# A small 32-bit matmul ahead of the third plain unit, and a new order of work, in an attention and two-layer kernel

## The chip, the cores and the metric

The kernel runs on one core of a Trainium2 chip. A core has engines that run side by side, each with its own queue of instructions: TensorE (PE in the profile; PEld is its loading of weights), VectorE (DVE), ScalarE (ACT), GpSimd (POOL) and SyncE (SP), which here only issues transfers. Sixteen DMA engines move data between the memory (HBM) and the core. Engines wait for each other by semaphores; within one engine the instructions are done in the order of its queue. The metric is the time of one execution on the device, in microseconds.

## The reference

Causal attention over 24 heads of 448 positions with 64 columns each, then two layers on the 896 x 768 result: a gated one and one with hardswish.

```python
scores = scale * np.matmul(q, k.transpose(0, 1, 3, 2))
scores = np.where(mask, -1000000000.0, scores)
attn = np.exp(scores - max); attn = attn / (sum + 1e-09)
x = (attn @ v) as (896, 768)
gate = 1.0 / (1.0 + np.exp(-(x @ w_gate)))      # 768 x 1536
x = (gate * (x @ w_val)) @ w_out                # 1536 x 768
h = x @ w_in                                    # 768 x 2048
out = (h * np.clip(h + 3.0, 0.0, 6.0) / 6.0) @ w_out2   # 2048 x 768
```

The weights come as 64-bit floats.

## The kernel before

**Numbers.** A 64-bit weight is loaded as two 32-bit words and turned into a 32-bit float by one ScalarE and four VectorE operations (`dec_scale`, `dec_shift`, `dec_clamp`, `dec_join`, `dec_sign`; tiles `raw` and `b`). Each operand of a product is split into a high part `hi` and a rest `lo`, both in the type that the profile calls fp32r; a product takes three matmuls (hi·hi, hi·lo, lo·hi). A split is done by ScalarE and VectorE (`split`), or by two ScalarE operations and a transfer that adds, issued by GpSimd (`dma_split`).

**Stages.** Attention comes first. Then the gated layer: four "plain units" (a unit is 128 columns of `w_gate` or `w_val`; 36 matmuls of 448 columns into accumulator `m`, line 994 and before), after that ten pairs of units by a scheme with seven products instead of eight (`Pairs`), which needs sums of the operand: T1 to T4, made in `tsum` tiles r11, r12, r21, r22 by eight sums `t_op(0)` to `t_op(7)` on VectorE and split into tiles `T`. The first pair multiplies the operand `x` by weights `g` (18 matmuls), then T2 by a weight sum `S` split into `hi` and `lo`, and so on, into accumulators `w`. Then `w_out` (accumulator `m`, tiles `y`), sixteen units of `w2_in` as eight pairs, and `w2_out` in two halves of 384 output columns, c = 0 and c = 1. Each half has seven tiles of 128 rows (`po[t]`), finished in the order 0, 2, 4, 6, 1, 3, 5, copied to `osb` and stored: half 0 by one transfer of all seven, half 1 by one transfer for each tile.

Two places already have a matmul of 64 x 64 in 32 bits on an accumulator that the next product overwrites: before the first product of `w_out`, and before the T2 product of the first pair of `w2_in`.

**Order.** Attention is issued by due times written in the kernel. After it every call is only noted (`Later`) and issued at the end by two tables. The steps of the four engines other than TensorE are numbered, ScalarE's first, then VectorE's, GpSimd's and SyncE's (966 to 1032). `ORDER` lists these numbers; `AHEAD` says how many of TensorE's steps, which keep the order of the program, come before each. Each engine's queue follows the table. Of SyncE's numbers 1023 is the store of half 0, and 1026 to 1032 are the stores of half 1's tiles t = 0, 2, 4, 6, 1, 3, 5.

Of the kernel before, what the change touches and what calls it, by code (L numbers as in the profile page):

```python
# [70 lines left out]
def kernel(  # L71
# [12 lines left out]
    nc = tc.nc  # L84
    B, H, S, D = q.shape
# [175 lines left out]
    with tc.manual_schedule():  # L261
        kept = ctx.enter_context(tc.tile_pool(name="kept", bufs=1))
        tsum = [kept.tile([P, 2, HK, S], F32, tag=f"q{2 + i}", name="tsum") for i in range(2)]
        r11, r12 = (tsum[0][:, i] for i in range(2))
# [377 lines left out]
        nc = Later(nc)  # L642
# [347 lines left out]
        def plain_unit(j):  # L990
            f, v = divmod(j, 2)
            if j < 2:
                ps = first_acc[j]
                halves(ps, at1[f, v], x_of, 0, True, True, (1,))
            else:
                ps = acc()
                halves(ps, at1[f, v], x_of, 0, True, True)
            plain[v] = ps
# [87 lines left out]
        for o in range(KD):  # L1086
            py = acc()
            if o == 0:
                t = g1[0][0].bitcast(F32)[:, :D]
# [144 lines left out]
        for c in range(2):  # L1234
# [105 lines left out]
        )  # L1340
        AHEAD = (
# [71 lines left out]
```

## Time and profile before

| | |
|---|---|
| median of three runs | 574.07 us (573.53 to 575.9) |
| the profiled execution, its own time | 573.63 us |
| its span, first to last instruction | 571.9 us |
| PE / PEld busy | 565.2 us (99%) / 500.2 us (87%) |
| DVE / ACT / POOL busy | 462.9 us (81%) / 344.5 us (60%) / 92.5 us (16%) |
| granted clock of TensorE | 1.00 of full speed (2.4 GHz) |
| moved by DMA | 84.57 MB |

A busy share is an average over stages with different limits. Which stage is bound by what is read from the chain of waits, which is followed back from the last instruction, and from the timeline of one engine. Matmuls overlap, so the duration of one is longer than the distance from its start to that of the next; the distance is what counts in a stream of them, and it is got from the start times of groups. Records of matmuls and of weight loads stand apart, and the load for a matmul runs beside the matmul before it.

### The profile page before, as it was taken

Reading aid. Unit: us, or ns where it says so; the run is one execution under the profiler, and the core shown is the slowest. Engines: PE = TensorE matmul, PEld = TensorE weight load, DVE = VectorE, ACT = ScalarE, POOL = GpSimd, SP = SyncE. Lnnn points to the kernel's source line nnn. Section 1 sums busy time; section 2 is a strip of 40 time slices with the busy share of each in tenths; the row PEclk is TensorE's granted clock in tenths of the full one; section 3 lists DMA queues with packets and bytes.
Section 4 is the critical chain, followed back from the end, with each engine's and each line's share of the span. In section 5 each row is a group of like instructions: output and inputs, shape, how many; then the busy total and the mean of one; then the engine's idle time right before and its main releaser. Section 6 shows DMA issues by size and latency. Waiting matters only on the chain.

```text
span 571.9 us, 8667 instructions
## 1 busy us (share of the span) xinstructions
PE 565.2 (99%) x3220; PEld 500.2 (87%) x3221; DVE 462.9 (81%) x706; ACT 344.5 (60%) x648; POOL 92.5 (16%) x152
## 2 busy tenths in 40 slices
PE   9999999999999999999999999999999999999997
PEld 5666656899999999999999999999999999999997
DVE  4789998897988998899878779899989999858201
ACT  4888888296667566686334439868768764333100
POOL 2545646021111110100000002212111000000000
PEclk9999999999999999999999999999999999999999
DMA  7756650389767686752644456898988153336002
GB/s 157 164 141 146 149 144 18 108 184 229 204 154 168 160 245 166 180 153 41 198 157 147 150 140 111 195 219 209 231 202 197 45 166 111 118 104 207 0 14 84
DMA packets 87785, 84.57 MB, mean 148 GB/s; under 512 B 35776, under 2 KB 77504, under 8 KB 87744
## 3 DMA queue, kind: packets, MB, share of 16 engines
q1 hardware_dynamic: 79904, 64.27, 37.9%
q0 software_dynamic: 6912, 19.53, 19.2%
q8 instruction: 25, 0.41, 0.3%
q10 hardware_dynamic: 928, 0.23, 0.2%
q14 instruction: 16, 0.13, 0.1%
HBM read 61.73 MB, written 2.75 MB: 113 GB/s over the span
## 4 chain that ended last, share of the span: by engine, by line
PE 90%; DVE 6%; ACT 2%; issue 1%; POOL 0%; DVEq 0%
PE w L46 40%; PE m L46 40%; PE pav L441 2%; PE pt L421 2%; PE s L367 2%; ACT pr L391 1%; DVE nm L379 1%; PE tr L334 1%; PE pt L533 1%; PE m L240 1%; DVE tsum L280 1%; DVE b L175 1%; DVE pth L431 1%; DVE raw L167 1%; DVE b L181 1%
## 5 line engine op out<-in xcount | busy, mean ns | idle before, releaser
L46 PE MATMUL m<-hi,g 128*128 128x384 f32 x448 | 113.9, 334 | 0.0
L46 PE MATMUL w<-T,hi 128*128 128x448 f32 x324 | 92.1, 366 | 0.0
L46 PEld LDWEIGHTS m<-hi,g 128*128 128x128 f32 x448 | 81.0, 188 | 0.0
L46 ACT ACTIVATE b<-raw 128x768 f32<-128x768 f32 x62 | 56.3, 914 | 37.9 <-DVE lo L46 18.2
L46 PE MATMUL m<-lo,g 128*128 128x384 f32 x224 | 74.8, 334 | 0.0
L46 PE MATMUL m<-g,hi 128*128 128x448 f32 x288 | 70.2, 366 | 0.0
L46 PEld LDWEIGHTS w<-T,hi 128*128 128x128 f32 x324 | 60.8, 188 | 4.9
L46 DVE SCALAR_TENSOR_TENSOR b<-raw,b 128x768 int32<-128x768 int32 x62 | 58.9, 954 | 1.0
L46 DVE SCALAR_TENSOR_TENSOR b<-b,raw 128x768 int32<-128x768 int32 x62 | 58.8, 954 | 0.9
L46 PE MATMUL w<-T,lo 128*128 128x448 f32 x162 | 59.2, 365 | 0.0
L46 PEld LDWEIGHTS m<-g,hi 128*128 128x128 f32 x288 | 54.0, 188 | 4.3
L411 POOL TENSOR_SCALAR pr<-pr,rc 128x192 f32<-128x192 f32 (+3 forms) x96 | 48.7, 525 | 49.2 <-DVE rc L403 40.4
L46 POOL DMA_DIRECT2D lo<-S x34 | 30.4, 898 | 152.9 <-ACT lo L46 98.2
L391 ACT ACTIVATE pr<-s,nm 128x192 f32<-128x192 f32 (+3 forms) x96 | 44.7, 479 | 4.7 <-DVE rc L403 2.5
L46 ACT CAST hi<-b 128x768 fp32r<-128x768 f32 x28 | 23.5, 838 | 38.4 <-DVE b L46 27.2
L46 DVE TENSOR_SCALAR b<-b 128x768 f32<-128x768 f32 x62 | 34.2, 555 | 12.9 <-ACT b L46 12.6
L46 PEld LDWEIGHTS m<-lo,g 128*128 128x128 f32 x224 | 42.0, 188 | 0.0
L46 PE MATMUL m<-g,lo 128*128 128x448 f32 x144 | 40.9, 365 | 0.0
L46 DVE TENSOR_TENSOR lo<-b,hi 128x768 fp32r<-128x768 f32 x28 | 26.6, 954 | 16.5 <-ACT hi L46 16.2
L46 DVE TENSOR_SCALAR raw<-raw 128x768 int32<-128x768 int32 x62 | 34.5, 560 | 4.6 <-DMA raw<-in_moe_w_in_dram 2.1
L46 PE MATMUL w<-x,g 128*128 128x448 f32 x180 | 38.2, 365 | 0.0
L46 ACT CAST g<-b 128x384 fp32r<-128x384 f32 (+1 forms) x36 | 23.9, 675 | 20.8 <-PE w L46 11.2
(124 smaller groups left out, 1086.4 us busy)
## 6 DMA issues: line engine op xcount, KB each, us to landing
raw<-in_moe_w_out_dram SPq DMA_DIRECT2D x28, 768.0 KB, 4.6
lo<-S POOLq DMA_DIRECT2D x34, 384.0 KB, 4.3
raw<-in_moe_w_in_dram SPq DMA_DIRECT2D x16, 768.0 KB, 5.7
raw<-in_moe_w_gate_dram SPq DMA_DIRECT2D x12, 768.0 KB, 5.3
raw<-in_moe_w_val_dram SPq DMA_DIRECT2D x12, 768.0 KB, 4.9
g<-b POOLq DMA_DIRECT2D x9, 384.0 KB, 6.3
q<-in_q_dram SPq DMA_DIRECT2D x24, 112.0 KB, 3.6
k<-in_k_dram SPq DMA_DIRECT2D x22, 112.0 KB, 3.7
```

The source lines that it names most:

```text
L46: steps.append((name, lambda: fn(*args, **kw)))
L167: nc.vector.tensor_scalar(lower, lower, 29, None, op0=ALU.logical_shift_right)
L175: nc.vector.scalar_tensor_tensor(bi, bi, 3, words(u)[1], op0=ALU.logical_shift_left, op1=ALU.bitwise_or)
L181: nc.vector.scalar_tensor_tensor(bi, words(u)[0], -(2 ** 31), bi, op0=ALU.bitwise_and, op1=ALU.bitwise_or)
L240: nc.tensor.matmul(ps[:, b, :S], lhsT=w[a][:, i * P : (i + 1) * P], rhs=x(c, k0 + i, b), start=(first and i == 0 and n == 0), stop=(last a ...
L280: op(r, a.bitcast(F32), b.bitcast(F32))
L334: nc.tensor.transpose(ps[:, c * CP : (c + 1) * CP], t[:, c].rearrange("p j d -> p (j d)"), identf[:CP, :CP],)
L367: nc.tensor.matmul(live["s", p, t][:, j], lhsT=live["qt", p][r, Q0[t] : Q0[t] + P], rhs=live["kt", p][r, : Q1[t]], start=False, stop=True, ...
L391: nc.scalar.activation(to if j else to[:, ::-1], ps[:, j].rearrange("p (c d) -> p c d", d=D), AF.Exp, bias=nm[:, j : j + 1], accum_out=sm[ ...
L411: nc.gpsimd.tensor_scalar(pr[:, j], pr[:, j], rc[:, j : j + 1], 1.0, op0=ALU.mult, op1=ALU.mult)
L421: nc.tensor.transpose(ps[:, o : o + P], live["pr", p, t].rearrange("p j n -> p (j n)")[:, c : c + P], identf,)
L441: nc.tensor.matmul(pav[r, Q0[i] :] if i else pav, lhsT=x[:, j] if i else x.rearrange("p j d -> p (j d)"), rhs=pt[g][:, off : off + w], sta ...
```

## The change

Before the product of the third plain unit (j == 2) a small matmul is put on the same accumulator. It reads 64 columns of r11, a 32-bit tile, as both operands, and the product overwrites what it writes. The two tables are new as a whole; their last rows are shown.

```diff
             else:
                 ps = acc()
+                if j == 2:
+                    t = r11[:, 0, :D]
+                    nc.tensor.matmul(ps[:D, 0, :D], lhsT=t, rhs=t, start=True, stop=True)
                 halves(ps, at1[f, v], x_of, 0, True, True)
             plain[v] = ps
...
-            909, 914, 368, 369, 371, 370, 1026, 915, 1029, 916, 1030, 1027, 1031, 1028, 917,
-            1032,
+            370, 1027, 1028, 1026, 915, 916, 371, 1030, 917, 1031, 1032, 1029, 1023,
```

TensorE's queue differs by the one matmul, between the second and the third plain unit (`x_73` is the last quarter of the attention's result, `x_70` the first, `m` the accumulator):

```order
 L46 MATMUL m<-x_73,hi 128x448 x2
 L46 MATMUL m<-x_73,lo 128x448
+L46 MATMUL m<-tsum 64x64
 L46 MATMUL m<-x_70,hi 128x448
 L46 MATMUL m<-x_71,hi 128x448
```

Nothing else in that queue moves.

VectorE's queue at the same time, before the change (`tsum_79` holds r11 and r12, `tsum_80` r21 and r22; the four rows that write `tsum` from `tsum` are t_op(4) to t_op(7)):

```order
L46 TENSOR_TENSOR tsum_80<-x11_73 128x1344
L46 TENSOR_TENSOR tsum_80<-tsum_80,tsum_79 128x1344
L46 TENSOR_TENSOR S_1747<-b_82 128x384
L46 TENSOR_SCALAR raw_1718<-raw_1718 128x768
L46 TENSOR_TENSOR S_1748<-b_81,b_82 128x384
L46 TENSOR_TENSOR S_1747<-S_1747,b_81 128x384
L46 TENSOR_SCALAR b_1754<-b_1754 128x768
L46 TENSOR_TENSOR tsum_79<-tsum_79 128x1344
L46 TENSOR_SCALAR b_1782<-b_1782 128x768
L46 TENSOR_TENSOR tsum_79<-tsum_80,tsum_79 128x1344
L46 TENSOR_SCALAR raw_1720<-raw_1720 128x768
L46 TENSOR_TENSOR tsum_80<-tsum_80,tsum_79 128x1344
```

and with it (`raw1_0_1741<-m_1685` is the gate product of the first two plain units):

```order
L46 TENSOR_TENSOR tsum_80<-x11_73 128x1344
L46 TENSOR_TENSOR tsum_80<-tsum_80,tsum_79 128x1344
L46 TENSOR_TENSOR tsum_79<-tsum_79 128x1344
L46 TENSOR_TENSOR tsum_79<-tsum_80,tsum_79 128x1344
L46 TENSOR_SCALAR raw_1718<-raw_1718 128x768
L46 TENSOR_TENSOR S_1747<-b_82 128x384
L46 TENSOR_SCALAR b_1754<-b_1754 128x768
L46 SCALAR_TENSOR_TENSOR b_1754<-b_1754,raw_1718 128x768
L46 SCALAR_TENSOR_TENSOR b_1754<-raw_1718,b_1754 128x768
L46 TENSOR_TENSOR tsum_80<-tsum_80,tsum_79 128x1344
L46 TENSOR_TENSOR raw1_0_1741<-m_1685,raw1_0_1741 128x896
L46 TENSOR_SCALAR raw_1720<-raw_1720 128x768
```

t_op(5) and t_op(6), which writes r11 last, have moved ahead of the weight work and the weight sums `S`; the gate product has moved ahead of the rest of the sums.

ScalarE's queue around the end of the first pair's first product, before the change (`raw1_0_1741<-w_1777` is the copy of that product out of its accumulator, `lo_1787` and `lo_1791` are splits for the second pair):

```order
L46 ACTIVATE raw1_0_1741<-m_1749 128x896
L46 ACTIVATE lo_1787<-raw1_3_1760 128x768
L46 CAST g_1784<-b_1782 128x384
L46 ACTIVATE lo_1791<-raw1_3_1760 128x768
L46 COPY raw1_0_1741<-w_1777 128x448
```

and with it:

```order
L46 ACTIVATE raw1_0_1741<-m_1749 128x896
L46 CAST g_1784<-b_1782 128x384
L46 COPY raw1_0_1741<-w_1777 128x448
L46 CAST hi_1761<-S_1748 128x768
L46 ACTIVATE lo_1787<-raw1_3_1760 128x768
```

The copy now stands ahead of both splits.

The end of SyncE's queue (`128x7x384` is the store of half 0, `128x384` that of a tile of half 1, `raw<-...` loads of weights):

```order
 L46 DMA raw<-in_moe_w_in_dram 128x6x128 x14
-L46 DMA raw<-in_moe_w_out_dram 128x2x384 x15
+L46 DMA raw<-in_moe_w_out_dram 128x2x384 x16
+L46 DMA out_dram<-osb 128x384 x7
 L46 DMA out_dram<-osb 128x7x384
-L46 DMA raw<-in_moe_w_out_dram 128x2x384
-L46 DMA out_dram<-osb 128x384 x7
```

The store of half 0 has moved from before the last load to behind all seven stores of half 1.

## Rows read from the trace of the kernel before

**Rows 1.** Chain of waits, from attention's end: start us, us, what
```profile
105.19 5.77 PE m L240 x27
110.96 22.32 PE m L46 x108
133.28 127.75 PE w L46 x630
261.02 88.01 PE m L46 x434
349.03 102.60 PE w L46 x506
451.63 116.52 PE m L46 x672
...
568.25 0.56 DVE osb L46
```

**Rows 2.** Timeline of TensorE's matmuls: start us, us, engine, line, operation, out<-in, tile, count
```profile
118.24 0.99 PE L46 MATMUL m<-x,hi 128*128 128x448 f32 x4
...
119.48 0.99 PE L46 MATMUL m<-x,hi 128*128 128x448 f32 x4
...
133.12 3.88 PE L46 MATMUL w<-x,g 128*128 128x448 f32 x18
136.83 0.56 PE L46 MATMUL w<-T,hi 128*128 128x448 f32 x2
...
206.14 3.81 PE L46 MATMUL w<-x,g 128*128 128x448 f32 x18
209.79 1.99 PE L46 MATMUL w<-T,g 128*128 128x448 f32 x9
```

**Rows 3.** The same view around the two small matmuls of before
```profile
259.04 1.98 PE L46 MATMUL w<-T,g 128*128 128x448 f32 x9
260.95 0.33 PE L46 MATMUL m<-g 128*64 128x64 f32 x2
...
262.53 0.97 PE L46 MATMUL m<-g,hi 128*128 128x448 f32 x4
...
352.61 0.33 PE L46 MATMUL w<-hi 128*64 128x64 f32 x2
```

**Rows 4.** Timelines of ScalarE and of weight loads at the first T2 product
```profile
135.35 0.84 ACT L46 ACTIVATE lo<-raw 128x768 fp32r<-128x768 f32 x1
136.09 0.52 ACT L46 COPY raw<-w 128x448 f32<-128x448 f32 x1
...
136.66 0.36 PEld L46 LDWEIGHTS w<-T,hi 128*128 128x128 f32 x2
```

**Rows 5.** Timeline of VectorE: t_op(4) and t_op(6)
```profile
111.97 1.56 DVE L46 TENSOR_TENSOR tsum<-tsum 128x1344 f32<-128x1344 f32 x1
...
117.72 1.55 DVE L46 TENSOR_TENSOR tsum<-tsum 128x1344 f32<-128x1344 f32 x1
```

**Rows 6.** Timelines of GpSimd and VectorE; in brackets idle time before, and its releaser
```profile
128.18 0.83 POOL L46 DMA_DIRECT2D lo<-S x1 [0.77 <-ACT lo L46]
...
137.63 0.56 DVE L46 TENSOR_TENSOR g<-b,g 128x384 fp32r<-128x384 f32 x1 [2.29 <-DMA lo<-S]
```

**Rows 7.** Stores: issue times (ns min/median/max, first and last start); KB and us to landing
```profile
L46 SPq DMA_DIRECT2D out_dram<-osb x8: 332/362/464, 516.5 to 568.8; - x8
...
out_dram<-osb SPq DMA_DIRECT2D x1, 1344.0 KB, 8.3
out_dram<-osb SPq DMA_DIRECT2D x7, 192.0 KB, 1.9
```

**Rows 8.** GB/s from 567 to 572 us in 40 slices; windows, GB/s last
```profile
GB/s 0 0 0 0 86 356 381 344 393 357 356 369 369 136 0 0 0 0 0 0 0 209 356 393 381 222 12 0 0 0 0 0 0 0 0 0 0 0 0 0
...
522.00:523.00 1.00, 1.00 (x8) 1.00 (x7) 0.85 (x1) 0.12 (x1) 0.00 (x0) 1.00 1.06 401
523.00:524.00 1.00, 1.00 (x8) 1.00 (x7) 0.19 (x1) 0.78 (x1) 0.00 (x0) 1.00 1.06 399
```

196 rows, old and new, of tables (AHEAD, ORDER) are left out of this document.

## The prediction

> **What bounds the kernel now.** I read the chain of waits first, because it says which engine the end hangs on at each time. The reader is to see in [rows 1] that up to 105 us it hops between engines (attention; its pieces are left out there), and that from 105.19 us to 568.15 us it is TensorE alone, without one piece of another engine or of waiting between. Then come only the last copy of a result tile on VectorE (0.56 us) and the stores. So 463 of 571.9 us are matmuls back to back. A change in the order on VectorE and ScalarE can gain nothing there; it can only lose, if an operand comes late. What can still change are three things: the number of matmuls, the distance from one matmul to the next, and what follows the last one.
>
> Second the timeline of TensorE, for that distance. It has two levels for 448 columns. In the four plain units it is 1.24 us for six, 206.7 ns (118.24 to 119.48) [rows 2]; later it is 3.65 us for 18, 202.8 ns (206.14 to 209.79) [rows 2]. The chain says the same over long pieces: 22.32 us for 108 is 206.7 ns, 127.75 for 630, 88.01 for 434 and 102.60 for 506 are each 202.8 ns [rows 1]. The granted clock is 1.00 (2.4 GHz) throughout, so this is not the clock. The step from one level to the other lies at 136.8 us, at the first matmul of the product with T2. That product accumulates into a bank which ScalarE must first copy out: the copy runs from 136.09 to 136.61 us, behind a 0.84 us operation that is not urgent, and the weight load starts at 136.66 us [rows 4], 0.03 us after its turn: a load starts with the matmul before its own, here the last of 18, at 133.12 + 17 x 0.2067 = 136.63 us. I take it that this little hold-up of the load put the stream of loads and matmuls into the closer spacing. That is argued, not shown.
>
> Third the stores: which transfer is issued last, how long it takes to land, and what rate stores reach [rows 7, 8].
>
> **The change part by part.** The sums are made against the profiled execution: span 571.9 us, 573.63 us in all. Its own time lies 0.44 us under the median of the three runs (574.07 us).
>
> *The small matmul.* Two of its kind are in the kernel already, each recorded as two matmuls of 64 columns. From 259.04 us, the first of nine, to 262.53 us lie 9 + 6 matmuls of 448 columns and the small one [rows 3]: 3.49 - 15 x 0.2028 = 0.45 us. TensorE has no idle time to hide it, so it costs +0.45 us.
>
> It also adds a wait: it reads r11, which is written last by the sum t_op(6). Queued behind it is everything TensorE does. In the old order that sum ran from 117.72 to 119.27 us [rows 5], and the third unit starts at 118.24 us; there it would have held TensorE up by 1.0 us. In the new order VectorE does t_op(4) to t_op(6) one behind the other: 111.97 + 1.56 + 2 x 1.55 = 116.6 us at the latest [rows 5]. So the wait is over 1.6 us before the matmul's turn and costs nothing.
>
> What may come back is the spacing. After both small matmuls of before the stream runs at 202.8 ns (the pieces from 261.02 and 349.03) [rows 1], though it did so before them too, so the trace does not show one turning the wide spacing into the close one. Both hold up a weight load, as the wait at 136.66 did, so I take it that the new one does turn it: two units of 36 matmuls and the 18 up to 136.8 us, 90 x 3.9 ns = -0.35 us. Bounds: 0 if it does nothing, and more than nothing lost if the later step goes missing (a rival below). [...]
>
> *The table, in the middle.* TensorE's row of work is unchanged but for the one matmul. Every operand that was in time with room stays in time, as far as I can follow it by hand; at the one place I worked through (rivals) about 2 us of room are left. I take 0, since no row of TensorE shows a wait there now, and above 0 as the bound.
>
> *The table, at the end.* This is the large term. SyncE's queue is served in order. In before the store of the first column half (128x7x384, 1344 KB) was issued at 516.5 us, under 50 us of matmuls. In the new table its number, 1023, is the very last, behind 1032, the store of the last tile, and behind 1029. The last tile is copied out at 568.81 us and its store was issued at 568.8 us [rows 1, 7]. So after that instant there are now three stores, 192 + 192 + 1344 KB, where there was one of 192 KB, and nothing is left to hide them.
>
> Issues on SyncE take 0.33 to 0.46 us each [rows 7], so the big one is issued at about 569.6 us, while the bytes of the first begin to move (0.8 us after its issue, at 569.6 in the fine view) [rows 8]. The queue then stays filled, and what counts is the extra 192 + 1344 KB = 1.573 MB by the rate. Small stores move at 344 to 393 GB/s in the busy slices of 0.125 us [rows 8]; while the big store was under way with a load beside it, two windows of 1 us show 401 and 399 GB/s [rows 8]. 1.573 MB / 400 GB/s = 3.9 us, at 369 GB/s 4.3 us. The time from the last byte to the end of the program is as before. I take +4.0 us. Bounds: at the highest rate of those slices for a store after another (393 GB/s) and with the start of the first bytes overlapped, 1.77 MB from 569.6 us would end 4.5 us later, at 574.1, against 570.4 in before: +3.7. From above: the big store took 8.3 us from issue to landing in before, with loads around it, the small one 1.9 [rows 7]: 569.6 + 8.3 - (568.8 + 1.9) = +7.2 us. The lower end is nearer to what happens with nothing else in the queue. The Trainium skill ("DMA: Bandwidth & Descriptors", section "Bandwidth") puts the limit of a core's traffic with HBM at about 358 GB/s; by that, an estimate, the term would be 4.4 us. The windows at 400 GB/s lie above it, so I keep 4.0.
>
> What the move frees at 516 us is worth nothing: TensorE waits for no load there [rows 1].
>
> *Sum:* +0.45 - 0.35 + 4.0 = +4.1 us: 577.7 us from the profiled execution's own time, 578.2 from the median. I write 577.9 us, 0.7% more than before.
>
> **The rivals.**
>
> 1. The close spacing is lost. In the new order ScalarE copies the first bank out ahead of the operations that held it up before, so the hold-up at 136.66 goes away. If the small matmul does not do in its stead what that did, the stream keeps 206.7 ns up to the next small matmul at 260.95 us: 612 matmuls x 3.9 ns = 2.4 us, and the 0.35 are not won. Sum 4.0 + 0.45 + 2.4 = +6.9, 580.6 us. For it: the reason of the step in before is an accident of order. Against it: after both small matmuls the spacing is the close one.
>
> 2. An operand comes late in the new order. Place: the rest of the second weight sum (the transfer lo<-S issued at 128.18 us), which VectorE saw landed at 137.63 us [rows 6] and TensorE needs first as the third matmul of the product with T3, 136.83 + 20 x 0.203 = 140.9 us. That is 3.3 us of room. Now VectorE's gate product, which needs a sigmoid that stands behind the copy of T2 on ScalarE, comes before the sums of that unit; I estimate the transfer's start 1 to 1.5 us later. It decides from 3.3 us; a miss by 1 to 3 us gives 579 to 581 us. Against: more than half the room is left.
>
> 3. Other side: not slower. The small matmul could bring a spacing below 202.8 ns that lasts. 1570 matmuls of 448 columns follow up to 451 us [rows 1]; 4.1 us are won back at 2.6 ns each, and from there the end store is paid for; at 199 ns it would be 573.63 + 4.1 - 1570 x 0.0038 = 571.8 us. For it only that two levels exist. Against it: both small matmuls left 202.8 ns as it was.
>
> 4. The end store costs less than I say: under 2.8 us the whole change would not be told from none. That needs 1.573 MB at 560 GB/s; no slice or window in [rows 8] shows more than 401. Time then about 576.3.
>
> **How the numbers follow.** A measurement of this kernel can tell about 0.5% (2.9 us) from no change: slower means over 576.9 us, faster under 571.2. Forecast 0.66; rival 1 0.13; rival 2 0.12; rival 3 0.03; rival 4 0.06. Slower: the forecast but for some hundredths in which the end store comes out at its lower bound and the runs fall low, and all of rivals 1 and 2: 0.87. Same: rival 4, these hundredths and half of rival 3: 0.11. Faster 0.02. The likeliest case alone spans 577.1 to 578.9 us. The range from 576.6 to 581.0 us takes in rivals 1 and 2 and the end store at up to 7 us, and leaves out rivals 3 and 4.
>
> **What would show it.** In the chain after: TensorE without a gap from 105 to about 568.3 us, then the copy, and the end some 4 us later than in before relative to it. In the list of stores the one of 1344 KB issued last, at about 569.7 us, and 350 to 400 GB/s in the stretch after the last matmul. On TensorE's timeline two matmuls of 64 columns at 118.2 us, and 202.8 ns from there on (206.7 would speak for rival 1, a piece of waiting between 105 and 568 us for rival 2). The prediction is wrong if the store of the half moves before the last matmul ends, or if its bytes take under 2.8 us.

## The result and the profile after

The changed kernel takes 578.00 us (median of 6 executions, 577.87 to 580.63), the kernel before, beside it on the same chip, 573.88 us (6 executions, 573.47 to 575.9): ratio 1.0075, 95% interval 1.0053 to 1.0096. It is slower, by 4.1 us; 577.9 us had been predicted.

The sum can be made from the two profiled executions (573.63 and 577.87 us; spans 571.9 and 575.9 us), piece by piece. The chain of waits of the changed kernel, columns as in [rows 1]:

```profile
104.87 5.77 PE m L240 x27
110.64 22.49 PE m L46 x110
133.12 127.68 PE w L46 x630
260.81 88.00 PE m L46 x434
348.81 102.60 PE w L46 x506
451.41 116.50 PE m L46 x672
...
568.00 0.56 DVE osb L46
```

As in [rows 1], there is no waiting and no other engine between attention and the last copy. The stretch of TensorE took 568.25 - 105.19 = 463.06 us before and 568.00 - 104.87 = 463.13 us now: +0.07 us for everything that was done in the middle. Attention, which the change leaves alone, happened to be 0.32 us shorter in this execution. After the last copy the old program ran from 568.81 us to 571.86 us, the new one from 568.56 to 575.94 us: 3.06 against 7.37 us, +4.32. So -0.32 + 0.07 + 4.32 = +4.07 us of span, and the tail is all of it.

The tail in detail: SyncE's timeline from 567 us (start, us, count), the stores and their median time to landing (columns as in [rows 7]), the bytes from 566 to 577 us in 40 slices of 0.275 us, and windows of 1 us (granted clock third from the end, GB/s last).

```profile
568.59 1.29 SPq L46 DMA_DIRECT2D out_dram<-osb  x3
```

```profile
out_dram<-osb SPq DMA_DIRECT2D x1, 1344.0 KB, 5.3
out_dram<-osb SPq DMA_DIRECT2D x3, 192.0 KB, 1.9
```

```profile
GB/s 0 0 0 0 39 352 319 6 0 0 0 0 184 363 363 279 341 374 374 363 385 357 380 369 363 374 380 374 374 363 73 0 0 0 0 0 0 0 0 0
```

```profile
571.00:572.00 1.00, 0.00 (x0) 0.00 (x0) 0.00 (x0) 0.00 (x0) 0.00 (x0) 1.00 1.00 372
572.00:573.00 1.00, 0.00 (x0) 0.00 (x0) 0.00 (x0) 0.00 (x0) 0.00 (x0) 0.52 1.04 372
573.00:574.00 1.00, 0.00 (x0) 0.00 (x0) 0.00 (x0) 0.00 (x0) 0.00 (x0) 0.50 1.03 373
```

Three stores are issued behind the last copy where [rows 7] had one, the big one last. After the copy every engine is idle (x0 throughout) and only bytes move: in the three windows from 571 to 574 us at 372 or 373 GB/s with nothing beside them, and the last of them in the slice that ends at 574.5 us. The extra 1.573 MB over 4.32 us is 364 GB/s, the few slower slices between the stores included.

The other end of the change is on TensorE's timeline around the small matmul, columns as in [rows 2]:

```profile
117.30 0.57 PE L46 MATMUL m<-x,hi 128*128 128x448 f32 x2
117.71 0.37 PE L46 MATMUL m<-x,lo 128*128 128x448 f32 x1
118.00 0.33 PE L46 MATMUL m<-tsum 128*64 128x64 f32 x2
118.26 1.08 PE L46 MATMUL m<-x,hi 128*128 128x448 f32 x4
119.18 0.57 PE L46 MATMUL m<-x,lo 128*128 128x448 f32 x2
119.59 0.97 PE L46 MATMUL m<-x,hi 128*128 128x448 f32 x4
120.40 0.57 PE L46 MATMUL m<-x,lo 128*128 128x448 f32 x2
```

Nothing stands in brackets, so it waited for nothing. From 117.71 to 119.18 us lie five matmuls of 448 columns and the small one: 1.47 - 5 x 0.2027 = 0.46 us. After it six take 120.40 - 119.18 = 1.22 us, 203 ns each; in the same place [rows 2] had 1.24 us, 206.7 ns.

### The profile page after: what moved, and what is told of

Its sections match the earlier page's. It is cut to its first block, busy times and chain, and to the rows that moved or that the text cites. A ratio compares the mean times of both kernels' runs of the same rounds, so it can differ in the third digit from the quotient of the medians.

```text
span 575.9 us, 8676 instructions
## 1 busy us (share of the span) xinstructions
PE 565.0 (98%) x3222; PEld 499.8 (87%) x3223; DVE 462.9 (80%) x706; ACT 344.8 (60%) x648; POOL 92.4 (16%) x152
## 4 chain that ended last, share of the span: by engine, by line
PE 90%; DVE 5%; ACT 3%; issue 1%; POOL 0%; DVEq 0%
PE w L46 40%; PE m L46 39%; PE pav L441 2%; PE s L367 2%; ACT pr L391 2%; PE pt L421 2%; PE tr L334 1%; DVE nm L379 1%; PE pt L533 1%; PE m L240 1%; DVE tsum L280 1%; DVE b L175 1%; DVE b L181 1%; PE s L359 1%; DVE pth L431 0%
## 5 line engine op out<-in xcount | busy, mean ns | idle before, releaser
L46 PEld LDWEIGHTS w<-x,g 128*128 128x128 f32 x180 | 33.8, 188 | 2.7
L46 PE MATMUL w<-T,g 128*128 128x448 f32 x162 | 35.8, 365 | 0.0
```

The lines of the kernel that those rows point to most:

```text
L46: steps.append((name, lambda: fn(*args, **kw)))
```

## The experiments

Each was timed beside the kernel before. "Tail" is the time from the end of the last copy to the end of the program.

**1. The store back in its place.** The changed kernel, with the store of half 0 issued ahead of the last load, in the table's numbers:

```diff
-... 360, 900, 1024, 894, 896, ...
+... 360, 900, 1024, 1023, 894, 896, ...
-... 1030, 917, 1031, 1032, 1029, 1023,
+... 1030, 917, 1031, 1032, 1029,
```

> The changed kernel with the store of half 0 moved back before the last load of weights, all else as changed. Theory A (the whole rise is the store at the end): 578.0 - 4.2 = 573.8 us, the same as before within 0.5 us; the last transfer is one tile of 192 KB and the span ends about 3.0 us after the last copy. Rival (the new order in the middle or the small matmul costs the time): it stays near 577 to 578 us.

Measured: 574.07 us (median of 12 runs), ratio to the kernel before 1.0004, with its 95% interval [0.9988, 1.0020]; tail 3.59 us. The whole rise is gone with one number of the table, so the rest of the new table and the small matmul together cost nothing that can be told. Of the tail 0.53 us above the old one are left, since tile 6's store (192 KB) still stands last.

**2. The store last, in the kernel before.** The reverse, and nothing else:

```diff
-... 898, 1024, 901, 902, 903, 1023, 361, ...
+... 898, 1024, 901, 902, 903, 361, ...
-... 1031, 1028, 917, 1032,
+... 1031, 1028, 917, 1032, 1023,
```

> The kernel before with only the store of half 0 moved behind the last tile's store. Theory A: 573.9 + 4.1 = 578.0 us (one small store fewer behind the last copy than in the changed kernel, 192 KB or 0.5 us less, so 577.5 to 578.0). Rival: 573.9 us.

Measured: 578.34 us (6 runs), ratio 1.0075 [1.0058, 1.0093]; tail 6.85 us. Three of the runs lie at 576.9 to 577.4 us and three at 579.3 to 579.7, so the median falls between two groups; the tail of the one profiled (577.35 us) is the surer figure. The store alone makes the kernel as slow as the whole change did. With experiment 1 there are three amounts: 192 KB more behind the last copy cost +0.53 us, 1344 KB +3.79 us, both together (the change) +4.32 us. The costs add up, at 363 to 371 GB/s.

**3. The changed kernel without the small matmul** (its result is overwritten, so nothing of the computation is left out):

```diff
-                if j == 2:
-                    t = r11[:, 0, :D]
-                    nc.tensor.matmul(ps[:D, 0, :D], lhsT=t, rhs=t, start=True, stop=True)
```

> The changed kernel without the small matmul, the table otherwise as changed (store last too). Theory A2 (a held-up weight load turns the spacing from 206.7 to 202.7 ns; in the new order nothing holds a load up at 136 us): the spacing stays 206.7 ns up to the next small matmul at about 260 us: -0.45 + 0.35 + 2.4 = +2.3 us, 580.2 us. Rival B (the first product with T2 turns it, whatever ScalarE does): it turns at 136.5 us as in before, -0.45 + 0.35 = -0.1 us, 577.8 us.

Measured: 578.23 us (6 runs), ratio 1.0084 [1.0067, 1.0100]. This decides nothing between the theories: its stream ran at 202.7 ns from 105 us on, so there was no wide spacing to be turned or kept. The profile shows something else. A stream that starts close, and has no small matmul in it, comes to the first pair earlier, and there it waits for ScalarE's copy (timeline of TensorE; in brackets the idle time and what ended it):

```profile
139.33 0.37 PE L46 MATMUL w<-T,lo 128*128 128x448 f32 x1
140.16 0.67 PE L46 MATMUL w<-T,hi 128*128 128x448 f32 x2 [0.47 <-ACT raw L46]
```

What the close spacing wins before 136 us is so given back at 140 us.

**4. The copy ahead of one split, in the kernel before.** ScalarE's copy of the first product (16) before the split lo_1791 (26):

```diff
-... 966, 22, 20, 26, 16, 400, ...
+... 966, 22, 20, 16, 26, 400, ...
```

> The kernel before with one step moved: ScalarE copies the first pair's first product out before the split that stood ahead of it, so the load for the T2 product is not held up. Theory A2: no turn at 136.8 us, 206.7 ns up to the small matmul at 261 us, 573.9 + 612 x 3.9 ns = 576.3 us. Rival B: it turns all the same, 573.9 us.

Measured: 573.03 us (12 runs), ratio 0.9994 [0.9979, 1.0009]. A miss: this stream, too, started close, so neither theory was put to the test, and the 0.96 us by which the median lies below the kernel before are not told from nothing by the interval. What the step does is seen against experiment 2, which also starts close and has the old order here: T2's product there, then here, on TensorE's timeline:

```profile
136.62 0.67 PE L46 MATMUL w<-T,hi 128*128 128x448 f32 x2 [0.72 <-ACT raw L46]
...
135.91 0.67 PE L46 MATMUL w<-T,hi 128*128 128x448 f32 x2
```

The 0.72 us of idle time before it are gone. By now the spacing at the start had been wide in two profiles (before, after) and close in four (experiments 1 to 4), among kernels whose instructions up to there are alike. So it is not set by what was edited.

**5. The small matmul in the old order.** The kernel before with the three lines of experiment 3 added, its tables as they were (but for one more TensorE step):

> The kernel before with the small matmul alone: its tables stay, so t_op(6), which writes the operand last, still ends at 119.27 us, while TensorE comes to the small matmul at 118.24 us. Theory A (the operand's wait is real in the old order, the rest as priced): a row of waiting of 0.6 to 1.2 us on VectorE at the small matmul, which the chain of the changed kernel does not have; +1.0 for it, +0.45 for the matmul, and where the stream began wide -0.35 for the spacing, less up to 0.6 us that TensorE would else have waited for the copy of the first product: +0.5 to +1.4 us, 574.4 to 575.3 us. Theory B (the new order gained nothing for this operand): no such row, +0.1 to +0.5, about 574.2 us. In both the tail after the last copy stays at 3.1 us and the end store is not among what is added.

Measured: 574.65 us (12 runs), ratio 1.0025 [1.0010, 1.0041]; tail 3.06 us. The list of TensorE's waits has the row that theory A asked for, and the timeline the place:

```profile
117.75 0.37 PE L46 MATMUL m<-x,lo 128*128 128x448 f32 x1
119.14 0.30 PE L46 MATMUL m<-tsum 128*64 128x64 f32 x2 [1.03 <-DVE tsum L46]
119.37 1.08 PE L46 MATMUL m<-x,hi 128*128 128x448 f32 x4
```

The wait is 1.03 us; 1.0 had been read from the end of t_op(6) at 119.27 us [rows 5]. Theory A holds: the small matmul needed the new order.

**6. The copy ahead of cast and split, in the kernel before.**

```diff
-... 966, 22, 20, 26, 16, 400, ...
+... 966, 22, 16, 20, 26, 400, ...
```

> The kernel before with ScalarE's copy of the first product's accumulator issued ahead of both the cast g_1784 and the split lo_1791, so that TensorE has nothing to wait for at T2's product. Theory A (those waits are all there is to gain): no row of waiting on ScalarE for the products with T2 and T3; the stretch of TensorE is shorter by what is waited there when the stream begins close, 0.2 to 1.0 us, and nothing when it begins wide: 572.6 to 573.9 us. Theory A2 (the hold-up at that copy is what turns a wide stream close): if the stream begins at 206.7 ns it stays there to the small matmul of w_out, 612 x 3.9 ns = 2.4 us, 576 us; if it begins at 202.7 ns this says nothing.

Measured: 572.90 us, ratio 0.9995 [0.9976, 1.0013]; 8 of 12 runs at 572.6 to 573.3 us and 4 at 575.7 to 575.8 us. No wait is left after 105 us, as theory A has it; the four long runs make the comparison as a whole a draw. Such a second group is in every kernel so far (in the one before 21 of 93 runs, some 2.2 us longer), and here it lies 3.0 us higher. The profile is from the first group and started close.

**7. The changed kernel mended.** Experiment 1, with tile 6's store ahead of tile 5's, and the copy of T2's product (19) ahead of the split lo_1787 (22):

```diff
-... 917, 1031, 1032, 1029,
+... 917, 1031, 1029, 1032,
-... 14, 22, 398, 967, 399, 923, 400, 23, 19, 29, ...
+... 14, 19, 22, 398, 967, 399, 923, 400, 23, 29, ...
```

> The changed kernel with three steps of the new table put right: the store of half 0 issued ahead of the last load again, the store of tile 6 ahead of that of tile 5, and ScalarE's copy of the product with T3's predecessor ahead of the split lo_1787. Theory A (sum of the terms): tail after the last copy 3.1 us in place of 7.4, no wait on ScalarE at the second pair of products, the small matmul still there: 572.8 to 573.8 us, so 4.2 to 5.2 us under the changed kernel and not to be told from the kernel before. Rival (the new table's middle costs more than I saw, hidden behind the end store): 574.5 us or more with the tail at 3.1 us.

Measured: 573.51 us (12 runs), ratio 0.9997 [0.9983, 1.0010]; tail 3.06 us, no wait after 105 us; 4.5 us under the changed kernel. Theory A holds, and no further loss was hidden behind the end store.

**8. Nine small matmuls in a row**, on experiment 1's kernel:

```diff
-                    nc.tensor.matmul(ps[:D, 0, :D], lhsT=t, rhs=t, start=True, stop=True)
+                    for _ in range(9):
+                        nc.tensor.matmul(ps[:D, 0, :D], lhsT=t, rhs=t, start=True, stop=True)
```

> The changed kernel with the store of half 0 back in its place (574.07 us) and the small matmul issued nine times in a row at the same place in place of once; eight more of a thing that was priced at 0.45 us. Theory A (each costs what the one costs): +8 x 0.45 = +3.6 us, 577.7 us. Theory B (0.45 us is the cost of going from 448-column matmuls to a small one and back, and a further one costs only its own two passes of 64 columns, 0.05 to 0.15 us): +0.4 to +1.2 us, 574.5 to 575.3 us. The stretch on TensorE's timeline from the first small matmul to the first of the third unit tells it apart: 0.26 us with one; 3.9 us by A, 0.7 to 1.5 us by B.

Measured: 575.05 us (12 runs), 0.98 us more than experiment 1. On the timeline:

```profile
117.96 0.37 PE L46 MATMUL m<-x,lo 128*128 128x448 f32 x1
118.26 1.26 PE L46 MATMUL m<-tsum 128*64 128x64 f32 x18
119.45 1.08 PE L46 MATMUL m<-x,hi 128*128 128x448 f32 x4
120.37 0.57 PE L46 MATMUL m<-x,lo 128*128 128x448 f32 x2
```

The first of them to the third unit is 1.19 us, theory B. From 117.96 to 120.37 us, less five large ones, are 1.40 us; eight more cost 0.94 us, 0.12 each. The one costs 0.46 us because it breaks the stream, not because of its own two passes.

This profiled execution was also the longest of its twelve (577.14 us, 2.1 us above their median), and so shows what one long run is made of. Its chain, and its timeline on both sides of the old small matmul at 353 us:

```profile
261.99 88.00 PE m L46 x434
350.00 104.51 PE w L46 x506
454.51 116.50 PE m L46 x672
```

```profile
349.83 3.82 PE L46 MATMUL w<-y,g 128*128 128x448 f32 x18
353.58 0.33 PE L46 MATMUL w<-hi 128*64 128x64 f32 x2
...
359.49 3.88 PE L46 MATMUL w<-y,g 128*128 128x448 f32 x18
363.21 2.02 PE L46 MATMUL w<-T,g 128*128 128x448 f32 x9
```

104.51 us in place of 102.60 [rows 1]. Before the small matmul, 18 take 353.58 - 349.83 = 3.75 us with the step into the small one; behind it 3.72 us, 206.7 ns each, and so on to 451 us. Here a small matmul has turned the close spacing into the wide one, for 1.91 us (104.51 against 102.60).

**9 to 11. Without the old small matmuls.** Theory A3 comes from that: the stream keeps the spacing it has until a small matmul or a late operand holds up a weight load, and then takes either. Experiment 9 is experiment 6 without both old small matmuls, experiment 10 experiment 6 without the second, experiment 11 experiment 7 without both, so that the new one is alone (their results are overwritten; nothing of the computation is left out):

```diff
             if o == 0:
-                t = g1[0][0].bitcast(F32)[:, :D]
-                nc.tensor.matmul(py[:D, 0, :D], lhsT=t, rhs=t, start=True, stop=True)
...
-                if self.ahead and p == 0:
-                    t = self.grp[p, 2][0].bitcast(F32)[:, :D]
-                    nc.tensor.matmul(
-                        self.banks[p][1][:D, :D], lhsT=t, rhs=t, start=True, stop=True
-                    )
```

> e6_copy_ahead (572.90 us, nothing in it that holds TensorE up from 105 to 451 us but the two old small matmuls) without those two small matmuls; their results are overwritten, so nothing of the computation is left out. Theory A3 (the stream keeps the spacing that it starts with until something holds up a weight load): 2 x 0.45 us less where it starts at 202.7 ns, 572.0 us, and where it starts at 206.7 ns it stays there for all 1701 matmuls of 448 columns, 1701 x 3.97 ns = 6.8 us more, about 578.8 us; two groups of runs some 6 to 7 us apart, none between 574 and 577 us. Theory B (the spacing changes by itself, and the runs that are 2 to 3 us longer come from elsewhere): the runs stay in two groups 2 to 3 us apart, 572.0 and 574.0 to 575.0 us.

> e6_copy_ahead without the second old small matmul alone, the one ahead of T2's product in the first pair of w2_in. Theory A3: 0.45 us less, 572.45 us, for a start at 202.7 ns; a start at 206.7 ns lasts from 105 us to the small matmul of w_out at 260 us, 765 x 3.97 ns = 3.0 us more, 575.5 us; no run in between at +1.9 us, which is what the profile with nine small matmuls showed from 353 to 451 us. Theory B (that piece of 206.7 ns does not come from the small matmul): runs at +1.9 us, about 574.4 us, among the twelve.

> e7_mended (573.51 us) without the two old small matmuls, so that the new one is the only one. Theory A3: 0.9 us less, 572.6 us, in the runs in which the new one leaves the stream at 202.7 ns; in the others the wide spacing lasts from 118 to 451 us, 1638 x 3.97 ns = 6.5 us more, about 579.1 us; none at +2 to +3 us. Theory B: 572.6 us and a few runs at +2 us, as e7_mended had.

Measured, 9: 573.87 us, ratio 0.9986 [0.9966, 1.0007], in three groups: 4 runs at 572.1 to 572.4, 6 at 573.8 to 574.3, 2 at 576.8 to 576.9 us. Neither theory had that. The profiled run (574.34 us) started close, and without the small matmul a tile T of VectorE's is late at 353 us (timeline of weight loads, then of matmuls):

```profile
353.06 0.19 PEld L46 LDWEIGHTS w<-T,hi 128*128 128x128 f32 x1 [0.34 <-DVE T L46]
```

```profile
357.30 3.88 PE L46 MATMUL w<-y,g 128*128 128x448 f32 x18
361.02 1.19 PE L46 MATMUL w<-T,g 128*128 128x448 f32 x5
```

Behind that hold-up 18 matmuls take 3.72 us: the wide spacing. A3's mechanism stands, its forecast failed for want of this place. A start at 206.7 ns that lasts to 353 us would cost some 1220 x 3.97 ns = 4.8 us, which is where the two longest runs lie; no profile shows one.

Measured, 10: 574.28 us, ratio 0.9997 [0.9977, 1.0017]; 4 runs at 572.4, 5 at 574.3 to 574.8, 2 at 575.4 to 575.5, and the profiled one at 577.49 us. That one started wide and nothing held it up before 260 us: ScalarE's copy of the first product ends at 135.42 us, ahead of T2's product at 136.55 us. The copy on ScalarE's timeline, the chain, and two places of TensorE's timeline:

```profile
134.89 0.53 ACT L46 COPY raw<-w 128x448 f32<-128x448 f32 x1 [2.59 <-PE w L46]
```

```profile
110.67 22.32 PE m L46 x108
132.99 130.20 PE w L46 x630
263.19 88.01 PE m L46 x434
351.20 104.28 PE w L46 x504
```

```profile
207.23 3.88 PE L46 MATMUL w<-x,g 128*128 128x448 f32 x18
210.95 1.40 PE L46 MATMUL w<-T,g 128*128 128x448 f32 x6
...
263.12 0.33 PE L46 MATMUL m<-g 128*64 128x64 f32 x2
```

18 take 3.72 us still at 207 us, and 130.20 us stand where 127.68 did: 4.0 ns on each of 630 matmuls. So T2's product does not turn a wide stream by itself. In the kernel before the same product had its load held up by 0.03 us [rows 4], and there the spacing changed: with this pair, one execution each, rival B of experiment 3 is out, and theory A2 fits. The small matmul of `w_out` at 263 us ends the wide stretch (88.01 us after it, the close value), and a late T at 356 us starts it again (104.28). The granted clock is the same in all three stretches, windows of that run:

```profile
110.00:250.00 140.00, 140.00 (x679) 127.14 (x678) 123.31 (x186) 91.83 (x131) 20.53 (x23) 1.00 0.75 187
264.00:350.00 86.00, 86.00 (x426) 79.72 (x425) 69.95 (x103) 37.61 (x54) 3.40 (x4) 1.00 0.50 143
```

The runs at 575.4 us are where A3 put a wide start. The five at +1.9 us are against its other half: that piece does not need the small matmul; the late T at the same place, which the profiles of experiments 9 and 10 show, does as well.

Measured, 11: 572.81 us, ratio 0.9968 [0.9954, 0.9982]; all 12 runs between 572.57 and 572.94 us. It is the one version that beats both kernels. Of A3's two groups only the short one came. In its profile the start is wide, the new small matmul turns the stream close, and a late T at 353 us leaves it close.

Over the 13 profiles the spacing changed ten times, and each time at a small matmul or at a load that was held up (by 0.03 to 0.34 us where no small matmul was). Where nothing of the kind stood, it never changed. Not every such place changes it: waits of 0.72 us (experiment 2) and 0.47 us (experiments 3 and 11) left a close stream close.

## Why the prediction was right, step by step

- **The end store.** Predicted +4.0 us (bounds 3.7 to 7.2), measured +4.32. The mechanism was right and stands shown by experiments 1 and 2; the rate was taken too high. That the whole sum (+4.1) still met the measured rise is in part luck: the 0.32 us by which attention was shorter in the profiled execution cover the 0.3 us by which the store was too cheap. The 401 and 399 GB/s of [rows 8] were windows with a load beside the store, while stores with nothing else move at 372 GB/s. Of the two rates that were weighed there, 369 GB/s from a full slice in [rows 8] gave 4.3 us. The limit of about 358 GB/s in the Trainium skill ("DMA: Bandwidth & Descriptors", section "Bandwidth") gave an estimate of 4.4 us, closer than the 4.0 chosen, though the windows of 372 GB/s lie above it.
- **The small matmul.** Predicted +0.45, measured +0.46.
- **Its wait.** Predicted none in the new order and 1.0 us in the old: none, and 1.03 (experiment 5). VectorE's three sums t_op(4) to t_op(6) now end at 116.4 us:

```profile
111.64 4.74 DVE L46 TENSOR_TENSOR tsum<-tsum 128x1344 f32<-128x1344 f32 x3
```

- **The turn of the spacing.** Predicted -0.35, together with the matmul +0.10; the stretch of TensorE grew by 0.07. In all five profiles in which a wide stream came to the new small matmul (after, experiments 5, 7, 8, 11) it left it close. The Trainium skill ("TensorE: Matmul & The Clock Gate", section "Back-to-back issue gap") gives columns / 2.4 + 2.5 ns as the gap of an isolated matmul, 189 ns for 448 columns, and says that a stream of weight loads and matmuls runs closer than that at 512 columns. The traces differ: the stream here runs at 202.7 or 206.7 ns, both above 189, in one program. That the term hangs on a wide start, which is not there in every execution, was not foreseen: where the start is close, the small matmul costs its 0.46 us and wins nothing. Two readings of the chain were loose there, and neither moves the sum: the 434 and 506 matmuls of [rows 1] hold two records of a small matmul each, and 1638 matmuls of 448 columns follow the new one up to 451 us (72 + 630 + 432 + 504), not 1570.
- **Rival 1, the close spacing lost.** The hold-up of [rows 4] is gone, as expected: the copy is done at 135.5 us, 1.1 us ahead of T2's product at 136.61 us (timeline of ScalarE):

```profile
134.99 0.53 ACT L46 COPY raw<-w 128x448 f32<-128x448 f32 x1 [0.29 <-PE w L46]
```

  The small matmul did in its stead what it had done. The rival did not come in the profiled run, but it is a real state: experiment 10's profile shows a wide stream kept to the next small matmul, at 2.52 us for 630 matmuls. Two of the changed kernel's six executions were 2.6 us longer than the rest, and 702 matmuls from 118 to 260 us at 3.97 ns make 2.8. That these two are rival 1 is not shown, since no profile of one was taken, and two things speak against it: in all five profiles with a wide start the new small matmul turned the stream, and experiment 11, which keeps it and leaves out the two old ones, has no long run among twelve. The other piece that was seen to turn wide, 504 matmuls from 353 us, would make 2.0 us.
- **Rival 2, an operand late.** No wait came up, but the working behind "1 to 1.5 us later" was wrong. The transfer of the rest of the second weight sum starts 3.65 us later than in [rows 6], beyond the 3.3 us of room given:

```profile
131.83 0.83 POOL L46 DMA_DIRECT2D lo<-S  x1 [4.02 <-ACT lo L46]
```

  What saved it is that it then took 4.2 us to land where it took 9.4 us before:

```profile
lo<-S POOLq DMA_DIRECT2D x1, 384.0 KB, 4.2
```

  It landed at 136.0 us, 1.5 us earlier than before. What lay beside it had moved too: the next transfer of its queue, lo<-raw, starts at 138.40 us in place of 132.88, and a load of weights (768 KB) that SyncE issued together with it before is now issued 1.6 us after it (SyncE's timeline, before and after):

```profile
128.17 0.37 SPq L46 DMA_DIRECT2D raw<-in_moe_w_val_dram  x1
...
133.40 0.37 SPq L46 DMA_DIRECT2D raw<-in_moe_w_val_dram  x1
```

  That these made it faster, and which of them, is argued; no run moved one alone. The conclusion held by luck of the queues, not by the room.
- **Rival 3, a spacing under 202.7 ns:** not in any of 13 profiles. **Rival 4, a cheap end store:** out, by the doses.

Open is what picks the spacing, at the start and after a hold-up. The places, the two levels and the price are shown; a cause is not. That the second group in the kernel before (some 2.2 us longer) is a wide stream kept to 260 us, 612 x 3.97 ns = 2.4 us, agrees with experiments 6 and 10 but was not caught in a profile; the piece from 353 us, 504 x 3.97 ns = 2.0 us, fits it as well.

## What to carry to other kernels

Follow the last entries of a new order before anything else: a store that stood under 50 us of matmuls cost its bytes divided by 363 GB/s as soon as it stood behind the last of them, while all the other moved steps and the small matmul together cost 0.07 us between the two profiled executions. Where a stream of matmuls bounds the kernel, read its spacing in every stretch, since two per cent of it can change at a hold-up of 0.03 us that no list of waits shows, and compare more than one execution. Room in time for a moved transfer must be worked out with what else then lies in the queue: here both its start and its duration moved by several microseconds, in opposite directions.

## What was not expected of the hardware

- The same matmuls with their weight loads run at 202.7 or at 206.7 ns for 448 columns at a granted clock of 1.00, hold the wide level over 155 us without a break (experiment 10), and in 13 profiles change it, either way, only at a hold-up or at a small matmul.
- A 64 x 64 matmul in 32 bits costs 0.46 us in a full stream, each further one behind it 0.12 us (experiment 8).
- Stores with nothing else under way add up linearly, 0.53, 3.79 and 4.32 us for 192, 1344 and 1536 KB, at 372 GB/s while they move.
- After the last matmul, which ends at 568 us, the granted clock falls to 0.50 (1.2 GHz) from 572 us on; nothing depended on it there.
